# P5 copied by ScalarE and P3's bank opened with P1+P6+P5 by VectorE, in the seven-product sets of a fused attention and MLP kernel

## The chip, the cores and the metric

The kernel runs on one core of one Trainium2 chip. The metric is the device time of one execution in microseconds (us), the median of several runs. Its engines are named as in the profile: PE is TensorE (matmul), PEld its weight load, DVE is VectorE, ACT is ScalarE, POOL is GpSimd, SP is SyncE.

## The reference

Linear attention with a decay per head, in blocks along the sequence, and then a two-layer MLP on its output:

```python
# q, k, v: (4 batches, 8 heads, 768 positions, 64), lam: one decay per head
for b in range(nb):                                   # blocks along the sequence
    intra = einsum('bhic,bhjc->bhij', qb, kb) * Dmask
    intra = einsum('bhij,bhjd->bhid', intra, vb)
    inter = einsum('bhid,bhde->bhie', qb * lam_pow, kv_state)
    out[:, :, sl] = intra + inter
    kv_state = lam_block * kv_state + einsum('bhsd,bhse->bhde', kb * rev_pow, vb)
x = out.transpose(0, 2, 1, 3).reshape(3072, 512)
h = x @ w_in                                          # 512 -> 2048
g = h * tanh(softplus(h))                             # Mish
return g @ w_out                                      # 2048 -> 512
```

## The kernel before

The sequence is cut into six stages `n` = 0 to 5 of 128 positions by 4 batches, 512 tokens each. The instructions of each engine stand in the order in which the program writes them (a manual schedule), so an engine that waits holds back all that is queued behind it. A stage runs the first layer, then the second (`fast_unit`), and in between pieces of the attention of the stage after it (`pair_a`, `pair_s`, `pair_o`), placed by hand in the dictionary `visit`.

The hidden layer has 16 tiles of 128 features. In stages 2 to 5, tiles 0 to 7 are computed plainly by eight calls of `mm1_duo(n, g, ...)`: two tiles by 256 tokens, 8 products of 128x256, into a bank of the PSUM tag `ph` (two banks), read by one Mish on ACT into `hsg`. Below, "the plain unit (g, h)" is pair `g` of the tiles and half `h` of the tokens. Tiles 8 to 15 are computed by two "sets", `g` = 0 and 1 (`set_unit`), each a 2x2 blocked product done with seven block products instead of eight (Winograd's form). A block product is 4 products of 128x256. With sums of blocks of the input (`xsum`, four DVE additions) and of the weights (`isum`), a set computes

- P1 and P2; Mish(P1+P2) gives block (0,0),
- P5, kept in SBUF as `p5`,
- P6 on top of P1 in bank z: z = P1+P6,
- P7 on top: z = P1+P6+P7; Mish(z+P5) gives block (1,1) (the sum goes through the SBUF tile `hs`),
- P3 into bank y, which starts as a copy of P1+P6; Mish(P1+P6+P3+P5) gives block (0,1),
- P4 on top of z; Mish(z) gives block (1,0).

The banks of the two sets are given by `homes`: x, z, w, y of set 0 lie in tags pS, pS, po, pk, those of set 1 in pk, po, ph, ph. w holds P5. In the code x is `sx0`/`sx1` in the profile, z is `sz`, w is `sw`, y is `sy`, the copy of P1 is `u`, `p5` is `p`.

The stage's list `units` sets the order. Unit 4 is the plain unit (0,1), preceded by `pair_s` of the next stage, whose four mask products (DVE, L365, tile `sb`) read the banks that z and y take over; after unit 4 come the four `xsum`. Units 5 to 12 are the plain units (1,1) and (2,1) with the steps "hold" and "open" (ACT copies P1 back into bank z), P5 and P6 of set 0, P5 and P6 of set 1, the plain unit (3,1), P7, P3 and P4 of both sets, and last the step "late", the Mish of y. Unit 13 starts the second layer with its P1 (tile `x`, needs plain tiles only); P5 of the second layer (tile `w`, weights `gsum`) follows. `token_sum` (DVE, tile `gsum`, placed by `sums`) makes sums over blocks of `hsg`: `gsum0` in two parts from block (1,1) of the plain tiles and of block (1,0) of the sets, then `gsum1`, `gsum3` and `gsum2`.

Of the kernel before, what the change touches and what calls it, by code (L numbers as in the profile page):

```python
# [9 lines left out]
AF = mybir.ActivationFunctionType  # L10
# [10 lines left out]
def kernel(  # L21
# [10 lines left out]
    nc = tc.nc  # L32
    B, H, S, D = q.shape
    C = 128
    NG = S // C
# [41 lines left out]
    def load_v(i):  # L77
        nc.gpsimd.dma_start(out=vz[i % NVB][:, :, 0:D], in_=chunk_rows(v, i))  # L78
# [212 lines left out]
    def next_state(n, p):  # L291

        nc.vector.tensor_tensor(
            out=state[p][(n + 1) % 2], in0=raws[n, p],
            in1=lbc.unsqueeze(1).unsqueeze(3).broadcast_to([128, 2, JP, D]), op=ALU.mult)
# [112 lines left out]
    def pace():  # L408
        nc.gpsimd.tensor_copy(paced, mark[-1])  # L409
# [75 lines left out]
    def i_quarter(g, r, c):  # L485

        t = win[g - 2]
        return t[:, r * KH : (r + 1) * KH, c * 256 : (c + 1) * 256]
# [27 lines left out]
    first = {}  # L516
# [3 lines left out]
    def set_unit(n, g, step):  # L520

        def place(key):
            if (n, g, key) not in first:
                tag, bufs = homes[g][key]
                first[n, g, key] = ps.tile([128, 2, 2 * C], F32, name=f"s{key}{g}", tag=tag, bufs=bufs)
            return first[n, g, key]

        def kept(key):
            first[n, g, key] = work.tile([128, 2, 2 * C], F32, name=key, tag=key, bufs=2)
            return first[n, g, key]  # L530

        def mish(r, c, src):
            ni = NKI // 2 + 4 * g + 2 * c
            dst = hsg[n][:, ni : ni + 2, r * 2 * C : (r + 1) * 2 * C]
            nc.scalar.activation(dst, src, AF.Mish)
            mark.append(dst[0:1, 0, 0:1])

        def plus_p5(key, out):
            nc.vector.tensor_tensor(out=out, in0=first[n, g, key], in1=first[n, g, "p5"], op=ALU.add)

        def x_quarter(r, c):
            return lambda kk: xt[n][:, c * KH + kk, r * 2 * C : (r + 1) * 2 * C]

        def x_part(i):
            return lambda kk: xsum[n, i][:, kk, :]

        def w_quarter_(r, c):
            return lambda kk, m: i_quarter(g, r, c)[:, kk, m * 128 : (m + 1) * 128]

        def w_part_(i):  # L550
            return lambda kk, m: isum[g][i][:, kk, m * 128 : (m + 1) * 128]

        if step == "hold":
            place("w")
            return
        if step == "open":
            nc.scalar.activation(place("z"), first[n, g, "u1"], AF.Copy)
            return
        if step == "late":
            mish(0, 1, first[n, g, "y"])  # L560
            return
        key, lhs, rhs = {
            "P1": lambda: ("x", w_quarter_(0, 0), x_quarter(0, 0)),
            "P2": lambda: ("x", w_quarter_(1, 0), x_quarter(0, 1)),
            "P6": lambda: ("z", w_part_(1), x_part(1)),
            "P5": lambda: ("w", w_part_(0), x_part(0)),
            "P7": lambda: ("z", w_part_(2), x_part(2)),
            "P3": lambda: ("y", w_quarter_(1, 1), x_part(3)),
            "P4": lambda: ("z", w_part_(3), x_quarter(1, 1)),
        }[step]()  # L570
        t = place(key)
        for m in range(2):
            for kk in range(KH):
                nc.tensor.matmul(  # L574
                    t[:, m, :], lhs(kk, m), rhs(kk),
                    start=(step in ("P1", "P5") and m == 0 and kk == 0), stop=(kk == KH - 1),
                    skip_group_check=True)
        if step == "P1":
            nc.scalar.activation(kept("u1"), t, AF.Copy)
        elif step == "P2":  # L580
            mish(0, 0, t)
        elif step == "P5":
            nc.vector.tensor_copy(kept("p5"), t)  # L583
        elif step == "P6":
            nc.scalar.activation(place("y"), t, AF.Copy)
        elif step == "P7":
            o = work.tile([128, 2, 2 * C], F32, name="hs", tag="hs", bufs=2)
            plus_p5("z", o)
            mish(1, 1, o)
        elif step == "P3":  # L590
            plus_p5("y", t)
        elif step == "P4":
            mish(1, 0, t)

# [61 lines left out]
    p5 = {}  # L656
# [102 lines left out]
    units = [(mm1_unit, (0, ni)) for ni in range(NKI)]  # L759
# [3 lines left out]
    sums = {3: ((2, 0),), 7: ((2, 1),), 11: ((0, 0), (1, 0), (3, 0)), 15: ((0, 1), (1, 1)), 16: ((3, 1),)}  # L763
# [35 lines left out]
    for n in range(1, NG):  # L799
        r, s, t = Pair(), Pair(), Pair()  # L800
        r.n, r.bs, s.n, s.bs, t.n, t.bs = n, (2, 3), n + 1, (0, 1), n + 1, (2, 3)
        def duo(g, half):
            return mm1_duo, (n, g, half * (GT // 2), (half + 1) * (GT // 2))

        def part(g, *steps):
            return [(set_unit, (n, g, step)) for step in steps]

        later = []
        if 1 < n < NG - 1:
            later += [lambda i=(n + 1) * B + b: load_v(i) for b in range(B)]  # L810
        if n < NG - 2:
            later += [lambda f=f, i=(n + 2) * B + b: f(i) for b in range(B) for f in (load_k, load_q)]
        if n == 1:
            units = [[duo(g, half)] for half in range(2) for g in range(NKI // 2)]
            visit = {11: (pair_s, s), 16: (pair_o, s), 21: (pair_a, s), 26: (pair_s, t), 29: (pair_o, t)}
            turns = {1: 9, 4: 10, 7: 11, 23: 12, 25: 13}
            slots = range(8, 16)
            sums = {9: ((2, 0),), 11: ((2, 1),), 13: ((0, 0), (1, 0)), 15: ((0, 1), (1, 1)), 20: ((3, 0),), 21: ((3, 1),)}
        else:
            units = [part(0, "P1") + part(1, "P1") + [duo(0, 0)], part(0, "P2") + part(1, "P2") + [duo(1, 0)],  # L820
                     [duo(2, 0)], [duo(3, 0)],
                     [duo(0, 1)], part(0, "hold") + part(1, "open") + [duo(1, 1)], part(0, "open") + [duo(2, 1)],
                     part(0, "P5", "P6"), part(1, "P5") + [(duo_bank, (n, 3, 1))] + part(1, "P6"), [duo(3, 1)],
                     part(0, "P7") + part(1, "P7"), part(0, "P3") + part(1, "P3"),
                     part(0, "P4") + part(1, "P4") + part(0, "late") + part(1, "late")]
            visit = {}
            if n < NG - 1:
                visit = {0: (pair_a, r), 3: (pair_s, s), 13: (pair_o, s), 22: (pair_s, t), 25: (pair_o, t)}
            if n < NG - 2:
                visit[17] = pair_a, s  # L830
            turns = {1: (n + 1) * B + 2, 2: (n + 1) * B + 3, 20: (n + 2) * B, 23: (n + 2) * B + 1}
            slots = range(4, 16)
            sums = {8: ((2, 0),), 12: ((0, 0), (0, 1), (1, 0), (1, 1)), 14: ((2, 1),), 18: ((3, 0),), 19: ((3, 1),)}
        steps = ("P1", "P5", "P6", "P2", "P7", "P3", "P4")
        units += [[(fast_unit, (n, step, blk))] for step in steps for blk in range(2)]
        scales = []
        for u, calls in enumerate(units):
            for fn, args in calls:
                fn(*args)
            if n == 1 and u == 0:  # L840
                turn(8)
                look_s(7)
            if n == 1 and u == 2:
                f = look_kv(7)
                look_o(7)
                f()
                next_state(1, 1)
            for _ in range({0: 1, 1: 1, 2: 2, 3: 1, 4: 1}.get(u, 0) if n == 1 else 0):
                pace()
                ahead.pop(0)()  # L850
            if later and u in slots:
                pace()
                later.pop(0)()
            for i, part in sums.get(u, ()):
                token_sum(n, i, part)
            if turns.get(u, NG * B) < NG * B:
                turn(turns[u])
            if u in visit:
                f, s_ = visit[u]
                s_.spare = ("po", "po") if u < 13 else ("pS", "pk") if f is pair_a else ("ph", "po")  # L860
                if f is pair_o and s_ is s and n > 1:
                    f(s_, scales)
                else:
                    f(s_)
            if n > 1 and scales and u in (15, 16, 17, 19):
                scales.pop(0)()
            if n > 1 and u == 4:
                for i in range(4):
                    x_sum(n, i)
# [30 lines left out]
```

## Time and profile before

| | |
|---|---|
| median of 3 runs | 200.87 us (200.67 to 201.45) |
| the profiled execution | 202.27 us, of which the profile's span is 200.5 us |
| granted TensorE clock | 1.00 |
| busy in the span | PE 190.2 us (95%), PEld 157.4, DVE 149.6 (75%), ACT 111.3 (55%), POOL 78.8 |

A row of the timeline gives the start and the length in us, the engine, the line, the operation with what it writes and reads, how many instructions of the kind stand in a row, and in brackets the idle time before them with what ended it. The end of a matmul is modelled, so for PE the starts are read: rows of 8 products of 128x256 start 0.87 us apart when nothing holds them. Instructions of one group on ACT or DVE overlap their neighbours, since the next one starts before the one in front has written its last result.

### The profile page before, as it was taken

Reading aid. Unit: us, or ns where it says so; the run is one execution under the profiler, and the core shown is the slowest. Engines: PE = TensorE matmul, PEld = TensorE weight load, DVE = VectorE, ACT = ScalarE, POOL = GpSimd, SP = SyncE. Lnnn points to the kernel's source line nnn. Section 1 sums busy time; section 2 is a strip of 40 time slices with the busy share of each in tenths; the row PEclk is TensorE's granted clock in tenths of the full one; section 3 lists DMA queues with packets and bytes.
Section 4 is the critical chain, followed back from the end, with each engine's and each line's share of the span. In section 5 each row is a group of like instructions: output and inputs, shape, how many; then the busy total and the mean of one; then the engine's idle time right before and its main releaser. Section 6 shows DMA issues by size and latency. Waiting matters only on the chain.

```text
span 200.5 us, 5119 instructions
## 1 busy us (share of the span) xinstructions
PE 190.2 (95%) x2049; PEld 157.4 (79%) x2049; DVE 149.6 (75%) x287; ACT 111.3 (55%) x230; POOL 78.8 (39%) x129
## 2 busy tenths in 40 slices
PE   7976999999999999999999999999999999999993
PEld 3643446878898998987998987998987988888882
DVE  7887679899944978888969787969787928237813
ACT  5693575242665431467791557780666880786530
POOL 7996333679396810008870008870008000000000
PEclk9999999999999999999999999999999999999999
DMA  8999999999999998659999869999759714500014
GB/s 129 144 146 185 207 206 200 157 168 170 205 119 172 168 134 181 173 94 92 128 112 195 167 142 99 134 122 182 224 99 115 47 26 134 157 3 2 0 56 157
DMA packets 112458, 26.82 MB, mean 134 GB/s; under 512 B 101554, under 2 KB 112434, under 8 KB 112434
## 3 DMA queue, kind: packets, MB, share of 16 engines
q0 software_dynamic: 77552, 13.37, 94.0%
q1 hardware_dynamic: 30848, 9.97, 26.6%
q10 hardware_dynamic: 4034, 3.15, 5.3%
q8 instruction: 16, 0.26, 0.6%
q14 instruction: 8, 0.07, 0.1%
HBM read 27.26 MB, written 6.29 MB: 167 GB/s over the span
## 4 chain that ended last, share of the span: by engine, by line
PE 80%; DVE 8%; DMA 5%; POOL 4%; issue 1%; ACT 0%; DVEq 0%; POOLq 0%
PE ph L453 17%; PE z L626 14%; PE x L626 10%; PE ph L418 7%; PE y L626 5%; PE w L626 5%; PE sz L574 4%; DMA vz<-in_v_dram 4%; PE sx L574 3%; PE pS L349 2%; DVE sb L365 2%; DVE p L583 2%; PE pO L376 2%; PE sy L574 2%; DVE xsum L514 1%; POOL kn L67 1%
## 5 line engine op out<-in xcount | busy, mean ns | idle before, releaser
L453 PE MATMUL ph<-xt,win 128*128 128x256 f16 x384 | 45.0, 273 | 1.6 <-DVE p L583 1.4
L453 PEld LDWEIGHTS <-win 128*128 128x128 f16 x384 | 37.1, 98 | 6.8 <-issue 2.4
L626 PEld LDWEIGHTS <-gsum 128*128 128x128 f16 x384 | 36.9, 98 | 4.8 <-DVE tsum L480 0.3
L460 ACT ACTIVATE hsg<-ph 128x512 f16<-128x512 f32 x48 | 28.7, 597 | 15.6 <-PE ph L453 15.3
L409 POOL COPY paced<-hsg 1x1 f16<-1x1 f16 x42 | 9.8, 233 | 56.4 <-ACT hsg L460 55.9
L626 PEld LDWEIGHTS <-hsg 128*128 128x128 f16 x272 | 26.0, 98 | 3.2
L626 PE MATMUL x<-wout,hsg 128*128 128x256 f16 x192 | 23.7, 273 | 0.0
L626 PE MATMUL z<-tsum,gsum 128*128 128x256 f16 x192 | 23.6, 273 | 0.0
L67 POOL DMA_DIRECT2D kn<-in_k_dram x23 | 20.6, 894 | 6.3 <-DMA win<-in_moe_w_in_dram 2.1
L78 POOL DMA_DIRECT2D vz<-in_v_dram x24 | 21.2, 887 | 4.4 <-DMA wout<-in_moe_w_out_dram 1.7
L75 POOL DMA_DIRECT2D qn<-in_q_dram x23 | 20.4, 887 | 6.0 <-DMA wout<-in_moe_w_out_dram 3.6
L365 DVE TENSOR_TENSOR sb<-pS,maskT 128x512 f16<-128x512 f32 x32 | 19.8, 682 | 1.9 <-PE pS L349 1.8
L612 DVE TENSOR_TENSOR gsum<-hsg 128x1024 f16<-128x1024 f16 x24 | 16.2, 687 | 4.8 <-ACT hsg L460 2.8
L683 ACT ACTIVATE osum<-z 128x512 f32<-128x512 f32 x5 | 3.0, 597 | 25.1 <-PE z L626 25.1
L265 DVE TENSOR_TENSOR ktil<-kn,lk 128x512 f16<-128x512 f16 (+1 forms) x22 | 14.6, 683 | 2.5 <-DMA kn<-in_k_dram 2.5
L288 DVE TENSOR_TENSOR raw<-pv,state 64x256 f32<-64x256 f32 x24 | 10.1, 422 | 8.0 <-PE pv L328 7.6
L418 PE MATMUL ph<-xt,win 128*128 128x512 f16 x64 | 14.5, 379 | 0.3 <-ACT xt L257 0.3
L574 PEld LDWEIGHTS <-isum 128*128 128x128 f16 x128 | 12.4, 97 | 2.3 <-issue 0.3
L430 ACT ACTIVATE hsg<-ph 128x512 f16<-128x512 f32 x16 | 9.6, 597 | 5.8 <-PE ph L418 5.8
L653 DVE TENSOR_TENSOR osum<-z,p 128x512 f32<-128x512 f32 x6 | 4.1, 689 | 10.8 <-issue 6.0
L626 PE MATMUL y<-wout,gsum 128*128 128x256 f16 x96 | 11.8, 273 | 0.0
L418 PEld LDWEIGHTS <-win 128*128 128x128 f16 x64 | 6.1, 97 | 7.3 <-issue 0.5
(114 smaller groups left out, 320.2 us busy)
## 6 DMA issues: line engine op xcount, KB each, us to landing
vz<-in_v_dram POOLq DMA_DIRECT2D x24, 128.0 KB, 4.6
out_dram<-osum SPq DMA_DIRECT2D x12, 256.0 KB, 2.9
kn<-in_k_dram POOLq DMA_DIRECT2D x23, 128.0 KB, 5.5
qn<-in_q_dram POOLq DMA_DIRECT2D x23, 128.0 KB, 6.0
out_dram<-osum ACTq DMA_DIRECT2D x11, 256.0 KB, 3.1
wout<-in_moe_w_out_dram POOLq DMA_DIRECT2D x4, 512.0 KB, 16.8
win<-in_moe_w_in_dram POOLq DMA_DIRECT2D x3, 512.0 KB, 11.2
win<-in_moe_w_in_dram POOLq DMA_DIRECT2D x2, 256.0 KB, 7.3
```

What stands on the lines that cost most here:

```text
L67: nc.gpsimd.dma_start(out=kn[i], in_=chunk_rows(k, i))
L75: nc.gpsimd.dma_start(out=qn[i], in_=chunk_rows(q, i))
L78: nc.gpsimd.dma_start(out=vz[i % NVB][:, :, 0:D], in_=chunk_rows(v, i))
L265: (nc.gpsimd if B + 1 < i < 2 * B else nc.vector).tensor_tensor(out=t, in0=kn[i], in1=bc(lk, 2, D), op=ALU.mult)
L288: nc.vector.tensor_tensor(out=raw[rs, b % 2, j0 : j0 + nj, :], in0=pv[rs, :, rs], in1=olds(rs), op=ALU.add)
L365: nc.vector.tensor_tensor(out=s.sb[m][t], in0=sc[m][t], in1=bc(maskT, 1, JP), op=ALU.mult)
L418: nc.tensor.matmul(ph_t[ni][:, lo:hi], w_in(ni, kc), xt[n][:, kc, lo:hi], start=(kc == 0), stop=(kc == NKC - 1),)
L453: nc.tensor.matmul(t[:, m, lo - half * h : hi - half * h], w_in(ni, kc), xt[n][:, kc, lo:hi], start=(m == 0 and kc == 0), stop=(kc == NKC ...
L460: nc.scalar.activation(hsg[n][:, 2 * g : 2 * g + 2, half * h : half * h + h], t, AF.Mish)
L574: nc.tensor.matmul(t[:, m, :], lhs(kk, m), rhs(kk), start=(step in ("P1", "P5") and m == 0 and kk == 0), stop=(kk == KH - 1), skip_group_c ...
L612: nc.vector.tensor_tensor(out=gsum[n, i][:, ks, :], in0=a, in1=b, op=op)
L626: nc.tensor.matmul(places(n, key)[:, blk, lo:hi], lhs(kk, blk), rhs(kk, lo, hi), start=(fresh and kk == 0 and blk == 0), stop=(kk == HK - ...
```

## The change

In stages 2 to 5:

- P5 is copied out of bank w by ACT instead of DVE.
- Bank y is no longer a copy of P1+P6 made by ACT. A new step "mid", on DVE, writes P1+P6+P5 into it (`plus_p5("z", place("y"))`). P3 is then added by PE, and Mish reads the bank directly; the in-place addition of P5 on DVE after P3, and the step "late", go.
- The order: "open" of set 0 comes before "open" of set 1, "hold" goes; then P5 of both sets, P6 of set 0, "mid" of set 0, P6 of set 1, the plain unit (3,1), "mid" of set 1, and P7, P3, P4. The bank of the plain unit (3,1) is now the one left by the plain unit (2,1), not the one that held P5 of set 1.
- The Mish operations on ACT are in the order hs, hs, sy, sy, sz, sz; before it was hs, hs, sz, sz, sy, sy.
- The first part of `gsum2` moves from unit 8 to unit 9, where DVE does it between "mid" of set 1 and the first `hs`.
- In stage 5 the plain unit (1,0) comes before P2 of the two sets instead of after.

```diff
-        if step == "hold":
-            place("w")
-            return
         if step == "open":
             nc.scalar.activation(place("z"), first[n, g, "u1"], AF.Copy)
             return
-        if step == "late":
-            mish(0, 1, first[n, g, "y"])
+        if step == "mid":
+            plus_p5("z", place("y"))
             return
...
         elif step == "P5":
-            nc.vector.tensor_copy(kept("p5"), t)
-        elif step == "P6":
-            nc.scalar.activation(place("y"), t, AF.Copy)
+            nc.scalar.activation(kept("p5"), t, AF.Copy)
...
         elif step == "P3":
-            plus_p5("y", t)
+            mish(0, 1, t)
...
-                     [duo(0, 1)], part(0, "hold") + part(1, "open") + [duo(1, 1)], part(0, "open") + [duo(2, 1)],
-                     part(0, "P5", "P6"), part(1, "P5") + [(duo_bank, (n, 3, 1))] + part(1, "P6"), [duo(3, 1)],
+                     [duo(0, 1)], part(0, "open") + [duo(1, 1)], part(1, "open") + [duo(2, 1)],
+                     part(0, "P5") + part(1, "P5"), part(0, "P6", "mid") + part(1, "P6"), [duo(3, 1)] + part(1, "mid"),
                      part(0, "P7") + part(1, "P7"), part(0, "P3") + part(1, "P3"),
-                     part(0, "P4") + part(1, "P4") + part(0, "late") + part(1, "late")]
+                     part(0, "P4") + part(1, "P4")]
+            if n == NG - 1:
+                units[0] += units[1].pop(),
...
-            sums = {8: ((2, 0),), 12: ...
+            sums = {9: ((2, 0),), 12: ...
```

More of the change, by code (lines that the diff above doesn't have):

```diff
@@ L832 @@
             slots = range(4, 16)
-            sums = {8: ((2, 0),), 12: ((0, 0), (0, 1), (1, 0), (1, 1)), 14: ((2, 1),), 18: ((3, 0),), 19: ((3, 1),)}
+            sums = {9: ((2, 0),), 12: ((0, 0), (0, 1), (1, 0), (1, 1)), 14: ((2, 1),), 18: ((3, 0),), 19: ((3, 1),)}
         steps = ("P1", "P5", "P6", "P2", "P7", "P3", "P4")
```

## The prediction

> **What bounds the kernel now.** I read the page first, then the waits, then the timeline of the part of a stage that the change touches.
>
> ```profile
> span 200.5 us, 5119 instructions
> ...
> PE 190.2 (95%) x2049; PEld 157.4 (79%) x2049; DVE 149.6 (75%) x287; ACT 111.3 (55%) x230; POOL 78.8 (39%) x129
> ```
>
> ```profile
> PE ph L453 <- DVE p L583: 1.4, 4, 0.4
> ```
>
> PE is busy 95% of the span, so only what makes PE wait, or lets it start sooner, moves the end. The last row (us in total, times, longest) is such a wait: the plain unit (3,1) waits in each of the four stages for DVE's copy of P5 of set 1, whose bank it takes. The timeline shows its whole price. This is stage 4:
>
> ```profile
> 148.05 2.48 DVE L365 TENSOR_TENSOR sb<-pS,maskT 128x512 f16<-128x512 f32 x4 [0.59 <-PE pS L349]
> ...
> 149.26 0.60 ACT L460 ACTIVATE hsg<-ph 128x512 f16<-128x512 f32 x1 [1.17 <-PE ph L453]
> 149.76 0.60 ACT L557 ACTIVATE sz<-u 128x512 f32<-128x512 f32 x1
> ...
> 150.91 0.60 PE L574 MATMUL sw<-xsum,isum 128*128 128x256 f16 x4
> ...
> 151.28 0.60 ACT L460 ACTIVATE hsg<-ph 128x512 f16<-128x512 f32 x1
> ...
> 151.41 0.60 PE L574 MATMUL sz<-xsum,isum 128*128 128x256 f16 x4
> ...
> 151.91 1.28 DVE L583 COPY p<-sw 128x512 f32<-128x512 f32 x2
> 152.09 0.58 ACT L585 ACTIVATE sy<-sz 128x512 f32<-128x512 f32 x1 [0.22 <-ACT hsg L460]
> 152.28 0.60 PE L574 MATMUL sz<-xsum,isum 128*128 128x256 f16 x4
> ...
> 153.11 0.68 DVE L612 TENSOR_TENSOR gsum<-hsg 128x1024 f16<-128x1024 f16 x1
> 153.24 1.03 PE L453 MATMUL ph<-xt,win 128*128 128x256 f16 x8 [0.36 <-DVE p L583]
> ...
> 154.11 1.04 PE L574 MATMUL sz<-xsum,isum 128*128 128x256 f16 x8
> ...
> 154.81 1.29 DVE L539 TENSOR_TENSOR hs<-sz,p 128x512 f32<-128x512 f32 x2 [1.02 <-issue]
> ...
> 155.53 1.23 ACT L535 ACTIVATE hsg<-hs 128x512 f16<-128x512 f32 x2 [0.62 <-DVE hs L539]
> ...
> 155.86 1.04 PE L574 MATMUL sz<-xt,isum 128*128 128x256 f16 x8
> ...
> 156.67 1.07 ACT L535 ACTIVATE hsg<-sz 128x512 f16<-128x512 f32 x2
> ...
> 157.28 1.29 DVE L612 TENSOR_TENSOR gsum<-hsg 128x1024 f16<-128x1024 f16 x2
> ...
> 157.62 1.09 ACT L535 ACTIVATE hsg<-sy 128x512 f16<-128x512 f32 x2
> ...
> 158.84 3.48 PEld L626 LDWEIGHTS <-gsum 128*128 128x128 f16 x32
> ...
> 158.95 1.91 PE L626 MATMUL w<-tsum,gsum 128*128 128x256 f16 x16
> ```
>
> The 8 products at 153.24 take until 154.11: 0.87 us, so 4 take 0.44. The last 4 before them start at 152.28 and should be followed at 152.72; the plain unit starts at 153.24, 0.52 late. A further 0.06 lies at 150.91 to 151.41. From 153.24 PE runs on without a gap to `w`, the second layer's P5, 5.71 us later. It can do so because the first `gsum`, which `w` needs, starts at 157.28 and is written by 157.97, 0.87 before its weight load at 158.84. That slack decides what the change is worth.
>
> **The steps measured here**, all for tiles of 128x512. From the start of 4 products to the DVE operation that reads them 0.70 (154.11 to 154.81), to an ACT one 0.68 (151.41 to 152.09). DVE: start to start 0.60 (two copies from 151.91, the next at 153.11), 0.69 each by the rows below. ACT: start to start 0.505 in the first chain (149.26 to 151.28, four steps). From the start of `hs` on DVE to its Mish 0.72 (154.81 to 155.53), of which 0.03 is beyond its length. The second Mish follows the second `hs`, 0.60 later (156.13); the next comes 0.54 after (156.67), then 0.475 each (156.67 to 157.62, two). From the start of the first `sz` Mish to the first `gsum` 0.61 (156.67 to 157.28). From the start of a `gsum` to the `w` product that waits for it I take 0.84: 0.69 for itself, 0.04 to reach PE (the second copy starts at 152.51, ends at 153.20, PE goes at 153.24), 0.11 from weight load to product (158.84 to 158.95).
>
> ```profile
> L583 DVE COPY p<-sw 128x512 f32<-128x512 f32 x8 | 5.3, 685 | 3.5 <-PE sw L574 3.4
> L539 DVE TENSOR_TENSOR sy<-sy,p 128x512 f32<-128x512 f32 x8 | 5.2, 690 | 0.0
> L585 ACT ACTIVATE sy<-sz 128x512 f32<-128x512 f32 x8 | 4.7, 582 | 2.1 <-PE sz L574 1.2 <-ACT hsg L460 0.9
> L672 ACT ACTIVATE p<-w 128x512 f32<-128x512 f32 x6 | 3.6, 598 | 4.2 <-PE w L626 4.2
> ```
>
> **What each edit costs by itself.** DVE loses eight copies of 685 ns (5.3 us in all); the eight "mid" additions replace the eight in-place additions at the same price: 685 to 690 ns bounds an addition from one bank into another from both sides. ACT swaps eight copies of 582 ns (bank to bank) for eight of 598 ns (bank to SBUF, the row of the second layer's `p`). PE does the same products. Neither engine's total bounds the time, so the worth lies in the order. The Trainium skill, ScalarE: Activation LUTs, Step-by-step: what each stage is for, says that a ScalarE write to PSUM is faster than one to SBUF, which speaks against moving ACT's copy there. By the rows that is 16 ns a copy, two copies a stage, 0.13 us over the kernel if all of it showed; the sum below takes 0.60 for the copy.
>
> **Stage 4, step by step.** The third mask product (DVE, L365) starts at 148.05 + 2 x 0.60 = 149.25 and ends at 149.94. Bank z of set 0 is the one it reads, so "open" of set 0, now first behind the Mish of 149.26, waits for it: 149.97, against 149.76 for the "open" that stood there. Behind it on ACT are queued two Mish operations, the other "open" and then P5's copy, four steps of 0.505: the copy starts at 151.99 and ends at 152.59. PE: P5 of both sets from 150.91, P6 of set 0 at 151.78 (8 products later), P6 of set 1 at 152.22, the plain unit (3,1) at 152.66. Its bank is that of the plain unit (2,1), whose Mish, one step ahead of P5's copy, ends at about 152.1: no wait. So the plain unit starts 0.58 sooner (153.24 to 152.66); the DVE copy that it waited for is gone.
>
> What is late next: "mid" of set 0 needs P5's copy (152.59 + 0.03 = 152.62) and P6 (151.78 + 0.70 = 152.48): it starts at 152.62 and ends at 153.31; "mid" of set 1 starts at 153.22 and ends at 153.91. P7 of set 0 comes at 153.53, of set 1 at 153.97: both find their banks read, the second by a hair. `gsum2` goes third on DVE, 153.82, and the first `hs` fourth, 154.42 (P7 alone would allow 153.53 + 0.70 = 154.23). P4 of set 1 at 155.71 meets the second `hs` ending at 155.71: 0.04 at most.
>
> On ACT follow the Mish of hs at 154.42 + 0.72 = 155.14, hs 155.74, sy 156.28, sy 156.76, sz 157.23, sz 157.71. The two sy now stand ahead of the sz for which the first `gsum` waits. It starts at 157.23 + 0.61 = 157.84, later by 0.56 than before, although PE is 0.58 ahead. `w` would be due at 152.66 + 5.71 = 158.37; it starts at 157.84 + 0.84 = 158.68. After 4 products (0.44) it needs the second half of `gsum0`, 0.61 behind the first (DVE's x2 row at 157.28 with 0.68 each): another 0.17. So `w` counts as started at 158.85, against 158.95: **the stage gains 0.10 of the 0.58**. Put shortly, `w` starts 4.43 after the first `hs`. Behind `w` nothing moves: P6 of the second layer, 1.75 later, finds `gsum1` written.
>
> ```profile
> 88.60 2.48 DVE L365 TENSOR_TENSOR sb<-pS,maskT 128x512 f16<-128x512 f32 x4 [0.59 <-PE pS L349]
> 93.80 1.03 PE L453 MATMUL ph<-xt,win 128*128 128x256 f16 x8 [0.37 <-DVE p L583]
> 99.50 1.69 PE L626 MATMUL w<-tsum,gsum 128*128 128x256 f16 x14
> ...
> 118.22 2.49 DVE L365 TENSOR_TENSOR sb<-pS,maskT 128x512 f16<-128x512 f32 x4 [0.59 <-PE pS L349]
> 121.21 0.60 PE L574 MATMUL sw<-xsum,isum 128*128 128x256 f16 x4
> 123.62 1.03 PE L453 MATMUL ph<-xt,win 128*128 128x256 f16 x8 [0.34 <-DVE p L583]
> 129.33 1.91 PE L626 MATMUL w<-tsum,gsum 128*128 128x256 f16 x16
> ...
> 177.30 0.60 ACT L460 ACTIVATE hsg<-ph 128x512 f16<-128x512 f32 x1 [0.28 <-PE ph L453]
> ...
> 178.85 0.60 PE L574 MATMUL sw<-xsum,isum 128*128 128x256 f16 x4
> 181.26 1.03 PE L453 MATMUL ph<-xt,win 128*128 128x256 f16 x8 [0.34 <-DVE p L583]
> ...
> 186.50 1.69 PE L626 MATMUL w<-tsum,gsum 128*128 128x256 f16 x14
> ```
>
> One more row for the other stages is from the chain of waits that ended last, in stage 5 (start, length):
>
> ```profile
> 172.70 1.07 PE sx L574 x8
> ```
>
> **The other stages.** Stage 2 has stage 4's distances (88.60, 93.80, 99.50 are each 59.45 before): 0.10. In stage 3 the mask products lie earlier against PE: "open" at 118.22 + 1.20 + 0.69 + 0.03 = 120.14, P5's copy 122.16 to 122.76, "mid" 122.79, `hs` 1.80 later 124.59, `w` 129.02 against 129.33: 0.31 of the 0.66 that PE gains before the plain unit (123.62 to 121.21 + 1.75 = 122.96). Stage 5 has no mask products. There P2's 8 products take 1.07 instead of 0.87, waiting for ACT's copy of P1; the plain unit (1,0) now covers that, and all behind moves up by 0.20 or 0.21: P5 at 178.64, the plain unit at 180.39, 0.87 sooner. ACT: Mish at 177.09, "open" 177.60, Mish 178.11, "open" 178.61, Mish 179.12, P5's copy 179.62, "mid" 180.25, `hs` 182.05, `w` 186.48 against 186.50: 0.02. Only the second layer's P1 lies before `w` there, so the wait is longest.
>
> Sum: 0.10 + 0.31 + 0.10 + 0.02 = 0.53 us. The profiled execution (202.27, span 200.5) would become 201.74; the median of the runs, 200.87, which is 1.40 below that execution, becomes **200.3**. Six chained distances of about 0.02 each in four stages make it 200.3 within 0.5.
>
> **The rivals.** *The wait does not come back*: the same gap stands four times on PE, a bank frees it, and the sums arrive in time. Then 0.58 + 0.66 + 0.58 + 0.87 = 2.69 are gained, 198.2 us; the bound of 0.5% (below) is passed if `w` waits 0.12 a stage less than worked out. The Trainium skill, Perfetto Trace Analysis, Optimization Strategy, says that the same bubble repeating on the engine that should be saturated can mean too few buffers, by which freeing the bank would recover it whole. The 0.5 us gap in all four stages fits that. Against it: ACT cannot begin the first of six Mish operations before `hs`, and `hs` cannot start before P7 + 0.70, so with everything ahead of it free the chain shortens by only 0.19 in stages 2 and 4 (154.42 to 154.23), 0.06 in stage 3 (124.59 to 122.96 + 0.87 + 0.70) and 0.09 in stage 5 (182.05 to 180.39 + 0.87 + 0.70): 1.06 in all with the 0.53. 0.20, since each measured distance may be off.
>
> *ACT's queue costs more than the bank gives*: "open" of set 0 stands first and waits for the third mask product, with two Mish operations and P5's copy behind it, and the two sy stand ahead of the sz. If ACT's start-to-start were its 0.60 length in both chains, that adds 4 x 0.095 + 0.06 + 2 x 0.125 = 0.69 to the way to the first `gsum`, 2.8 in four stages, and 0.53 less makes 203.1 us. It turns slower than before from 0.13 a stage, and passes the bound of 0.5% from 0.38. For it: a first copy into a bank behind a wait isn't in these rows in this order. Against it: both cadences are measured on the same shapes. 0.12.
>
> *The plain unit still waits*, for the Mish of the unit (2,1) instead of a copy: by the sum that ends at 152.1, 0.5 before it is wanted. That would leave about 200.9, inside the forecast's case.
>
> **How the numbers follow.** A difference of 0.5% (1.0 us) is about what a measurement of this kernel can tell from no change. The forecast, 0.53 faster within 0.5, lies inside it: same 0.68. Faster by more 0.20, slower by more 0.12. The range 199.2 to 201.4 leaves out the far part of the faster case (0.08) and the slower case beyond 201.4 (0.12). The forecast's own range is 199.8 to 200.8.
>
> **What would show it.** Right: no wait of PE on P5's copy at L453, the plain unit (3,1) directly behind P6; a new idle of PEld before `w`, ended by DVE's `gsum`, of 0.3 to 0.7 a stage; sz Mish as the last of six, and `gsum` directly behind it. Wrong: `w` following the second layer's P1 without a gap (first rival), or PE idle before P7 with DVE's "mid" as its releaser (second).

## The result and the profile after

The changed kernel takes 200.61 us (median, 200.0 to 201.23), the kernel before 201.24 in the same comparison: a ratio of 0.9966 with a 95% interval of 0.9952 to 0.9981, that is 0.7 us faster (0.4 to 1.0). The forecast was 0.53 us faster, and 200.3 us within 0.5. A second comparison, e8 below, gave 0.9976 (0.9954 to 0.9998).

The page and the waits (us in total, times, longest) of the changed kernel:

```profile
span 199.1 us, 5098 instructions
...
PE 191.6 (96%) x2049; PEld 157.5 (79%) x2049; DVE 144.8 (73%) x279; ACT 110.8 (56%) x230; POOL 80.8 (41%) x129
```

```profile
PEld L621 <- DVE gsum L607: 2.7, 8, 0.7
...
PE w L621 <- DVE gsum L607: 0.4, 1, 0.4
```

The wait of PE on P5's copy is gone from the list. In its place stands the wait of the weight load on `gsum`, twice in each of the four stages: the second layer's P5 is now held. The timeline of stage 4, the rows that answer to those of before:

```profile
146.93 2.49 DVE L365 TENSOR_TENSOR sb<-pS,maskT 128x512 f16<-128x512 f32 x4 [0.59 <-PE pS L349]
...
148.14 0.60 ACT L460 ACTIVATE hsg<-ph 128x512 f16<-128x512 f32 x1 [1.17 <-PE ph L453]
...
148.91 0.60 ACT L554 ACTIVATE sz<-u 128x512 f32<-128x512 f32 x1 [0.17 <-DVE sb L365]
...
149.80 1.03 PE L571 MATMUL sw<-xsum,isum 128*128 128x256 f16 x8
...
150.67 1.04 PE L571 MATMUL sz<-xsum,isum 128*128 128x256 f16 x8
150.92 1.08 ACT L580 ACTIVATE p<-sw 128x512 f32<-128x512 f32 x2
...
151.54 1.04 PE L453 MATMUL ph<-xt,win 128*128 128x256 f16 x8
151.55 1.30 DVE L539 TENSOR_TENSOR sy<-sz,p 128x512 f32<-128x512 f32 x2 [0.67 <-ACT p L580]
...
152.41 1.08 PE L571 MATMUL sz<-xsum,isum 128*128 128x256 f16 x8
...
152.75 0.68 DVE L607 TENSOR_TENSOR gsum<-hsg 128x1024 f16<-128x1024 f16 x1
...
153.33 1.04 PE L571 MATMUL sy<-xsum,win 128*128 128x256 f16 x8
153.35 1.28 DVE L539 TENSOR_TENSOR hs<-sz,p 128x512 f32<-128x512 f32 x2
...
154.07 1.23 ACT L535 ACTIVATE hsg<-hs 128x512 f16<-128x512 f32 x2 [0.86 <-DVE hs L539]
...
155.21 1.07 ACT L535 ACTIVATE hsg<-sy 128x512 f16<-128x512 f32 x2
...
156.16 1.09 ACT L535 ACTIVATE hsg<-sz 128x512 f16<-128x512 f32 x2
...
156.79 1.29 DVE L607 TENSOR_TENSOR gsum<-hsg 128x1024 f16<-128x1024 f16 x2 [2.16 <-ACT hsg L535]
157.54 0.33 PEld L621 LDWEIGHTS <-gsum 128*128 128x128 f16 x4 [0.32 <-DVE gsum L607]
157.54 2.08 PE L621 MATMUL w<-tsum,gsum 128*128 128x256 f16 x16
...
158.14 2.95 PEld L621 LDWEIGHTS <-gsum 128*128 128x128 f16 x28 [0.27 <-DVE gsum L607]
...
159.47 1.91 PE L621 MATMUL z<-tsum,gsum 128*128 128x256 f16 x16
```

The plain unit (3,1) at 151.54 follows P6 (150.67) after 8 products' 0.87 us: no gap. DVE stands idle for 2.16 us before `gsum`, since ACT does the two sy (155.21) ahead of the sz (156.16) that `gsum` reads; with the sz first (e1 below) it is 1.18. PE's weight load waits twice.

**Measured by stage.** What stands ahead of the first set differs between profiles by more than the change moves: P1 of stage 2 starts at 82.16 before, 81.46 after, and between 80.83 and 83.22 in the experiments, although no edit touches what lies ahead of it. So the kernels are compared by the distances between the starts of P1 (`sx`) of stages 2 to 5, and in stage 5 from P1 to the second layer's P6. These are the rows of the changed kernel:

```profile
81.46 1.04 PE L571 MATMUL sx<-xt,win 128*128 128x256 f16 x8
...
110.97 1.04 PE L571 MATMUL sx<-xt,win 128*128 128x256 f16 x8
...
140.49 1.04 PE L571 MATMUL sx<-xt,win 128*128 128x256 f16 x8
...
169.56 1.04 PE L571 MATMUL sx<-xt,win 128*128 128x256 f16 x8
...
186.91 0.82 PE L621 MATMUL z<-tsum,gsum 128*128 128x256 f16 x6
```

All kernels, in us, with the timed ratio beside them (its 95% interval in brackets):

| kernel | stage 2 | 3 | 4 | 5 | sum against before | timed ratio |
|---|---|---|---|---|---|---|
| before | 29.62 | 29.83 | 29.18 | 17.46 | | |
| changed | 29.51 | 29.52 | 29.07 | 17.35 | -0.64 | 0.9966 (0.9952, 0.9981) |
| e8: changed, again | 29.51 | 29.51 | 29.06 | 17.35 | -0.66 | 0.9976 (0.9954, 0.9998) |
| e1: Mish of sz first | 29.13 | 29.14 | 28.68 | 16.59 | -2.55 | 0.9888 (0.985, 0.9927) |
| e2: gsum2 behind hs | 29.22 | 29.21 | 29.35 | 17.23 | -1.08 | 0.9932 (0.9896, 0.9968) |
| e3: stage 5 in the old order | 29.51 | 29.51 | 29.07 | 17.55 | -0.45 | 0.9983 (0.9965, 1.0001) |
| e4: P5 copied by DVE | 29.95 | 29.94 | 29.50 | 17.60 | +0.90 | 1.0051 (1.0025, 1.0078) |
| e5: before, other bank only | 29.10 | 29.10 | 28.65 | 16.95 | -2.29 | 0.9898 (0.9861, 0.9936) |
| e6: e1 and e2 | 29.09 | 29.09 | 28.63 | 16.60 | -2.68 | 0.9868 (0.9842, 0.9894) |
| e7: e5 and stage 5's order | 29.10 | 29.10 | 28.68 | 16.75 | -2.46 | 0.9878 (0.9842, 0.9913) |
| e9: open in the old order | 29.35 | 29.33 | 28.90 | 17.35 | -1.16 | 0.9967 (0.9948, 0.9985) |

The sums of the stages and the ratios (1% is 2.0 us) agree within the intervals, save for e9, which falls just outside. There is one profile for each kernel (two for the changed one, which agree within 0.01 a stage), and two waits for the DMA of `xt` are in the table that no edit touches. One, of 0.17 us, stands in stage 3 of the kernel before, which is 0.21 longer than its stage 2; in every other kernel stages 2 and 3 agree within 0.02. All sums count these 0.21. Without them the change gains 0.43 and e9 0.95, which lies within its interval (0.3 to 1.05). The other, of 0.63 us, stands in stage 4 of e2.

### The profile page after: what moved, and what is told of

The parts are those of the page before. It is cut to its first block, busy times and chain, and to the rows that moved or that the text cites. A ratio compares the mean times of both kernels' runs of the same rounds, so it can differ in the third digit from the quotient of the medians.

```text
span 199.1 us, 5098 instructions
## 1 busy us (share of the span) xinstructions
PE 191.6 (96%) x2049; PEld 157.5 (79%) x2049; DVE 144.8 (73%) x279; ACT 110.8 (56%) x230; POOL 80.8 (41%) x129
## 4 chain that ended last, share of the span: by engine, by line
PE 88%; ACT 5%; DVE 4%; issue 1%; ACTq 0%
PE ph L453 20%; PE z L621 14%; PE x L621 10%; PE ph L418 7%; PE w L621 6%; PE y L621 6%; PE sz L571 4%; PE sx L571 4%; PE pS L349 2%; PE pO L376 2%; PE pO L255 2%; PE sw L571 1%; ACT hsg L535 1%; PE pv L328 1%; PE sy L571 1%; PE busy L157 1%
## 5 line engine op out<-in xcount | busy, mean ns | idle before, releaser
L621 PEld LDWEIGHTS <-gsum 128*128 128x128 f16 x384 | 36.2, 98 | 7.3 <-DVE gsum L607 2.7
L409 POOL COPY paced<-hsg 1x1 f16<-1x1 f16 x42 | 11.9, 284 | 54.8 <-ACT hsg L460 54.5
L621 PE MATMUL w<-tsum,gsum 128*128 128x256 f16 x96 | 12.2, 273 | 0.6 <-DVE gsum L607 0.4
```

Source lines behind the costliest of these rows:

```text
L621: nc.tensor.matmul(places(n, key)[:, blk, lo:hi], lhs(kk, blk), rhs(kk, lo, hi), start=(fresh and kk == 0 and blk == 0), stop=(kk == HK - ...
```

## The experiments

**e1: where the gain went.** The changed kernel with the Mish of y behind P4 again:

```diff
+        if step == "late":
+            mish(0, 1, first[n, g, "y"])
+            return
...
         elif step == "P3":
-            mish(0, 1, t)
...
-                     part(0, "P4") + part(1, "P4")]
+                     part(0, "P4") + part(1, "P4") + part(0, "late") + part(1, "late")]
```

> The changed kernel, with the Mish of y put back behind P4 (step late), so that ACT does hs, hs, sz, sz, sy, sy. Theory A (the bank's gain is taken back because two sy Mish stand on ACT ahead of the two sz for which the first gsum, and with it the second layer's P5, waits): the chain from the first hs to P5 of the second layer is 0.95 us shorter a stage, P5 is no longer held, and 2.6 us against before are gained (stage gains 0.58, 0.66, 0.58, 0.87 less 0.04 each in two of them), about 2.0 more than the change. Theory B (the chain is bound by where hs starts, through the P5 copy and gsum2 on DVE, and ACT's order is only a part): P5 still held, at most 0.2 a stage more than the change, 1.2 to 1.4 us against before.

Measured: ratio 0.9888, 2.3 us; the stages show 2.55. Stage 4 of e1, by the timeline:

```profile
151.96 1.28 DVE L539 TENSOR_TENSOR hs<-sz,p 128x512 f32<-128x512 f32 x2
...
153.81 1.06 ACT L535 ACTIVATE hsg<-sz 128x512 f16<-128x512 f32 x2
154.42 1.29 DVE L608 TENSOR_TENSOR gsum<-hsg 128x1024 f16<-128x1024 f16 x2 [1.18 <-ACT hsg L535]
154.76 1.08 ACT L535 ACTIVATE hsg<-sy 128x512 f16<-128x512 f32 x2
...
155.83 2.72 PEld L622 LDWEIGHTS <-gsum 128*128 128x128 f16 x25
155.94 1.91 PE L622 MATMUL w<-tsum,gsum 128*128 128x256 f16 x16
```

`gsum` starts 2.46 after `hs` (3.44 in the changed kernel) and is written 0.72 before its weight load at 155.83, which no longer waits. Theory A holds, B falls: ACT's order alone held back 1.9 of the 2.55 us. The timed ratios say the same, as the intervals of e1 and of the changed kernel lie apart.

**e5: the bank alone.** The kernel before, with the banks of two tiles exchanged: the plain unit (3,1) and bank y of set 1. P6 of set 1 leaves its copy into y out (a step "copy" behind the unit makes it), and the unit's Mish is held back so that ACT keeps its order:

```diff
-    def mm1_duo(n, g, lo, hi):
+    def mm1_duo(n, g, lo, hi, later_mish=None):
...
+        if step == "copy":
+            nc.scalar.activation(place("y"), first[n, g, "z"], AF.Copy)
+            return
...
-                     part(0, "P5", "P6"), part(1, "P5") + [(duo_bank, (n, 3, 1))] + part(1, "P6"), [duo(3, 1)],
+                     part(0, "P5", "P6"), part(1, "P5", "P6"),
+                     [(mm1_duo, (n, 3, GT // 2, GT, held))] + part(1, "copy") + [(lambda held=held: held.pop()(), ())],
```

> The kernel before, with one thing changed: the plain unit (3,1) takes the bank left by the plain unit (2,1), and bank y of set 1 the one left by P5 of set 1 (the copy of z into y is written behind the unit's products and ahead of its Mish). All operations and ACT's order as before. Theory A: the unit follows P6 without a gap, the 0.50 to 0.52 us of each stage are gained, and the second layer's P5 is not held, since sz stands ahead of sy on ACT: 2.0 us faster than before, three times what the whole change gives. Theory B (what follows is bound by hs anyway): PE is held at P5 of the second layer instead, 0.5 us or less.

Measured: ratio 0.9898, 2.1 us; by the stages 0.52, 0.73, 0.53 and 0.51. Stage 4:

```profile
150.22 0.60 PE L582 MATMUL sz<-xsum,isum 128*128 128x256 f16 x4
150.66 1.04 PE L453 MATMUL ph<-xt,win 128*128 128x256 f16 x8
...
154.09 1.06 ACT L540 ACTIVATE hsg<-sz 128x512 f16<-128x512 f32 x2
...
154.70 1.29 DVE L621 TENSOR_TENSOR gsum<-hsg 128x1024 f16<-128x1024 f16 x2
...
156.26 0.75 PEld L635 LDWEIGHTS <-gsum 128*128 128x128 f16 x7
```

The unit comes 0.44 behind the last four products, and `gsum` (written by 155.39) lies 0.87 ahead of its load. Two exchanged banks, with one copy written later and no operation added, removed or given to another engine, give three times what the whole change gives. The old wait was worth its full 0.5 us a stage, as long as the order of the Mish operations stayed. Stage 3's 0.73 holds the 0.21 of the DMA's wait: 0.12 lies ahead of P5, the rest between P5 and P6.

**e4: who copies P5.** The changed kernel with `nc.vector.tensor_copy(kept("p5"), t)`.

> The changed kernel, with P5 copied by DVE again (all else as changed). Theory A: two copies of 0.60 stand on DVE ahead of mid, gsum2 and hs, so hs starts 0.45 us later in stages 2 to 4 and 0.26 in stage 5, P7 waits 0.3 for mid, and all of it reaches the end: 1.6 us slower than the change, 1.0 slower than before. Rival (which engine copies P5 is immaterial, the bank and the order do it all): as the change, 0.6 faster than before.

Measured: ratio 1.0051, 1.0 us slower than before. By the stages 0.44, 0.42, 0.43 and 0.25 more than the change, where 0.45 and 0.26 were expected. Stage 4:

```profile
152.47 1.04 PE L571 MATMUL sw<-xsum,isum 128*128 128x256 f16 x8
...
153.41 1.28 DVE L580 COPY p<-sw 128x512 f32<-128x512 f32 x2
...
154.61 1.29 DVE L539 TENSOR_TENSOR sy<-sz,p 128x512 f32<-128x512 f32 x2
...
156.40 1.29 DVE L539 TENSOR_TENSOR hs<-sz,p 128x512 f32<-128x512 f32 x2
```

`hs` starts 3.93 after P5 (153.35 - 149.80 = 3.55 in the changed kernel), 0.38 later; the other 0.05 of this stage lies ahead of P5 (152.47 is 9.36 behind P1, against 9.31). In stages 2, 3 and 5 `hs` is 0.43, 0.43 and 0.24 later. In the new order the copy's place on ACT is needed: what `hs` is late by is paid in full, since the second layer's P5 is what waits for it.

**e2: the sum that moved with it.** The changed kernel with `sums = {10: ((2, 0),), ...}`: `gsum2` behind both hs.

> The changed kernel, with the first part of gsum2 moved from unit 9 to unit 10, behind both hs. Theory A: hs starts when P7 allows, 0.19, 0.06, 0.19 and 0.09 us sooner in stages 2 to 5, and all of it reaches the second layer's P5, which is what is waited for: 0.5 us more than the change, 1.1 to 1.2 against before. Rival (ACT's six Mish are bound by ACT or by P3 and P4, not by the first hs): no more than the change, 0.6 against before.

Measured: ratio 0.9932, 1.4 us. Stages 2, 3 and 5 are 0.29, 0.31 and 0.12 shorter than the change; stage 4 shows a wait of 0.63 us for the DMA of `xt` that the change's profile doesn't have, and can't be compared:

```profile
147.19 2.78 PE L453 MATMUL ph<-xt,win 128*128 128x256 f16 x24 [0.63 <-DMA xt<-xtok]
```

Theory A holds in kind, and was low. In stage 2 of e2 `hs` starts 0.64 after P7, not the 0.70 worked out; in the changed kernel it starts 0.94 after P7 (94.32 and 93.38), not 0.89. So it is 0.30 sooner, where 0.19 was expected, and the stage is 0.29 shorter:

```profile
93.41 1.08 PE L571 MATMUL sz<-xsum,isum 128*128 128x256 f16 x8
...
94.05 1.29 DVE L539 TENSOR_TENSOR hs<-sz,p 128x512 f32<-128x512 f32 x2 [0.21 <-PE sz L571]
```

In stage 3 0.06 was expected, as the mask products were taken to lie earlier there than in stage 2; without the DMA's wait of before they don't, and stage 3 gains what stage 2 gains. The timed intervals of e2 and of the changed kernel overlap, so this rests on the stages.

**e3: stage 5's order.** The changed kernel without `units[0] += units[1].pop(),`.

> The changed kernel, with the plain unit (1,0) of stage 5 put back behind P2 of the sets. Theory A: P2 waits 0.2 us for ACT's copies of P1 again, all that follows in stage 5 starts from there, so 0.2 slower than the change and 0.4 to 0.5 faster than before; stages 2 to 4 keep their lengths of 29.5, 29.5 and 29.1 us between their P1. Rival (the second layer's P5 is held in stage 5 anyway, so the 0.2 is hidden): as the change.

Measured: ratio 0.9983, against 0.9976 for the changed kernel beside it (201.04 and 201.03 us), which can't tell 0.2 us. The traces can: stage 5 is 17.55 us, 0.20 longer, and the others as in the change. P2's 8 products start at 171.28, 1.03 after the plain unit, and the next starts 0.92 later:

```profile
170.25 1.04 PE L453 MATMUL ph<-xt,win 128*128 128x256 f16 x8
171.28 1.09 PE L571 MATMUL sx<-xt,win 128*128 128x256 f16 x8
172.20 5.40 PE L453 MATMUL ph<-xt,win 128*128 128x256 f16 x48
```

**e6 and e7: the best of both.** e6 is e1 with e2's place of `gsum2`; e7 is e5 with stage 5's order of the change.

> The kernel of e1 (Mish of y behind P4) with the first part of gsum2 in unit 10, behind both hs. Theory A: the second layer's P5 isn't held any more in e1, so the earlier hs only takes away what P4 waits for hs in stages 2 to 4 (its 8 products 0.92 instead of 0.87 us): 0.1 us or nothing on top of e1's 2.3 to 2.5 against before. Rival (the two are independent and add up): 0.5 more than e1.

> The kernel of e5 (before, the plain unit (3,1) on the bank left by (2,1)) with stage 5's plain unit (1,0) ahead of P2, as in the change. Theory A: the 0.2 us of P2's wait in stage 5 come on top: 2.2 to 2.3 us faster than before.

Measured: 0.9868 (198.99 us) and 0.9878 (198.8 us), 2.7 and 2.5 us faster than before, which the timing doesn't tell apart. By the stages e6 is 0.13 shorter than e1, not 0.5: with the second layer's P5 no longer held, an earlier `hs` is worth only what P4 waited for the second `hs` (in stage 4 P4's 8 products take 0.87, 153.46 to 154.33, against 0.92 in e1, 152.81 to 153.73). P7 takes 0.92 in both. e7 is 0.17 shorter than e5, all of it in stage 5 (16.95 to 16.75, with 0.03 lost in stage 4).

**e8: the changed kernel again.**

> The changed kernel as it is, beside the others on the same chip: 0.6 us faster than before by its trace (stages of 29.5, 29.5, 29.1 us between their P1, against 29.6, 29.8, 29.2, and 0.1 in stage 5).

Measured: ratio 0.9976, 0.5 us; by the stages 0.66, each within 0.01 of the first profile.

**e9: open behind the third mask product.** The changed kernel with `part(1, "open") + [duo(1, 1)], part(0, "open") + [duo(2, 1)]`.

> The changed kernel, with the two steps open in the old order (set 1 first), so that ACT doesn't stand behind the third mask product at the head of its queue. Theory A: in stages 2 to 4 P5's copies leave ACT 0.28 us sooner, mid is then bound by P6 and starts 0.18 sooner, and hs and the second layer's P5 with it: 0.5 us faster than the change, 1.1 faster than before; stage 5, without mask products, keeps its length. Rival (ACT catches up behind open, the place of open is immaterial): as the change, 0.6 faster than before.

Measured: the stages are 0.16, 0.19, 0.17 and 0.00 shorter than the change, as expected; the timed ratio is 0.9967, 0.7 us, which neither shows the 0.5 nor excludes it. Stage 4:

```profile
148.78 0.60 ACT L554 ACTIVATE sz<-u 128x512 f32<-128x512 f32 x1
...
149.94 1.03 PE L571 MATMUL sw<-xsum,isum 128*128 128x256 f16 x8
...
150.77 1.09 ACT L580 ACTIVATE p<-sw 128x512 f32<-128x512 f32 x2
...
151.52 1.30 DVE L539 TENSOR_TENSOR sy<-sz,p 128x512 f32<-128x512 f32 x2 [0.50 <-PE sz L571]
```

P5's copy starts 0.83 after P5 (1.12 in the changed kernel), and "mid", now released by P6, 1.58 after it (1.75). The mechanism is in the trace; that it moves the time by 0.5 us isn't shown.

## Why the prediction was right, step by step

- **The wait and its end.** The plain unit (3,1) follows P6 at once in all four stages. e5 shows that the gap was worth what the timeline said, about 0.5 (0.52, 0.53 and 0.51 in stages 2, 4 and 5).
- **What is late next.** The chain named, P5's copy on ACT, "mid", `gsum2`, `hs`, six Mish, `gsum`, is the one in the trace. From P5 to `hs` 3.51 was worked out for stage 4, 3.55 measured; from `hs` to the first product of `w` 4.26 and 4.19 (153.35 to 157.54); the second wait 0.17 and 0.18 (159.47 - 157.54 - 1.75). Stage 4 gained 0.11 against 0.10, stage 2 the same. That it is so close is in part luck, as two small errors cancel. The first "open" was put 0.03 behind the end of the third mask product and comes about 0.09 behind it (148.91, against 146.93 + 1.20 + 0.69 = 148.82). And from the start of `gsum` to `w` 0.84 was taken, 0.11 of it from weight load to product; where the load itself waits, load and product start together (157.54), and it is 0.75 (156.79 to 157.54).
- **Stage 5** gained 0.11, not 0.02. The terms are the same surplus between `hs` and `w`, here 0.08, and 0.02 ahead of `hs`; there is no mask product here to cancel them:

```profile
177.42 1.04 PE L571 MATMUL sw<-xsum,isum 128*128 128x256 f16 x8
...
180.81 1.28 DVE L539 TENSOR_TENSOR hs<-sz,p 128x512 f32<-128x512 f32 x2
...
184.99 2.09 PE L621 MATMUL w<-tsum,gsum 128*128 128x256 f16 x16 [0.42 <-DVE gsum L607]
```

  `hs` is 3.39 after P5 (3.41 worked out), `w` 4.18 after `hs` (4.26).
- **Stage 3** came out at the forecast's 0.31, but about 0.2 of it lies in the kernel before and not in the change. From P5 (`sw`) to the second layer's P6 the gain is 0.20 (121.21 to 131.08 before, the 129.33 of `w` and 1.75; 120.28 to 129.95 after). The other 0.12 lies ahead of P5 (9.43 and 9.31 from P1): before, PE waited there for the DMA of `xt`, after it didn't. The forecast took the mask products' lead over P5 in stage 3 (121.21 - 118.22 = 2.99) as fixed; it held that wait, and is 2.87 after (120.28 - 117.41). The row of before (stage 3's plain unit (0,1), with the idle time in brackets):

```profile
118.59 2.78 PE L453 MATMUL ph<-xt,win 128*128 128x256 f16 x24 [0.17 <-DMA xt<-xtok]
```

  From P5 on the sum is 0.11 + 0.20 + 0.11 + 0.11 = 0.53. That this is the forecast's figure is luck: stage 5 gave 0.09 more and stage 3 0.11 less. Had the kernel before not waited for the DMA, stage 3 would by its stage 2 have gained 0.10, and the whole 0.43 (an estimate: 29.62 in place of 29.83). One profile of before can't say how often it waits there.
- **The small waits.** P4 was to wait at most 0.04 for the second `hs`; P7, whose wait was put at nothing ("by a hair"), and P4 take 0.92 and 0.91 in place of 0.87 in stages 2 to 4 (152.41 to 153.33, 154.21 to 155.12). They cost nothing there, since the second layer's P5 is held behind them; e6 against e1 shows P4's as 0.13 us in all.
- **ACT's copy.** The groups of the changed kernel have it at 604 ns, 22 more than the copy into PSUM (582) that it replaces:

```profile
L580 ACT ACTIVATE p<-sw 128x512 f32<-128x512 f32 x8 | 4.3, 604 | 0.0
```

  The rule of the Trainium skill that writing to PSUM is faster for ScalarE (ScalarE: Activation LUTs, Step-by-step: what each stage is for) agrees in sign. e4 shows that it doesn't decide who should copy: the copy on VectorE, whose queue is on the chain, costs 1.5 us more by the stages.
- **The rivals.** The first (the wait doesn't come back) didn't occur in the change, but is what e1 shows once ACT's order is put back: 2.55 us by the stages where 2.69 was worked out. The rule of the Trainium skill weighed with it, that a repeated bubble can mean too few buffers (Perfetto Trace Analysis, Optimization Strategy), points at the right place: e5 gains the whole gap with the banks alone. But e5 adds no buffer, two tiles only exchange theirs, so too few buffers isn't what the gap showed. The change gained about a quarter of e5's, as the new ACT order let PE wait at another place. The second rival (ACT slower than its cadence) is excluded by the cadences: open to P5's copy 4 steps in 2.01 us (148.91 to 150.92), sy to sz two steps in 0.95 (155.21 to 156.16). The third (the plain unit still waits) didn't occur either.

## What to carry to other kernels

When a wait of the bound engine is removed, look for the slack of the next thing that it needs, here 0.87 us at `gsum`, and ask whether the same edit makes that later: an order on a second engine that is busy only 56% of the span took back three quarters of the gain. Among operations that become ready together on such an engine, do those first that somebody waits for soonest, even if that keeps a bank longer. And try the smallest part of a change alone: here the exchange of two banks, in e5, was worth more than the whole.

## What the runs showed that was not expected

Whether PE waits for the DMA of `xt` differs between profiles: 0.17 us in stage 3 before, none in the changed kernel, 0.63 in stage 4 of e2. The part ahead of the sets, which no edit touches, ends between 80.83 and 83.22 us. Both make a single profile's span a poor measure of a change below 1 us: e9's span equals the changed kernel's 199.1, while its stages are 0.5 shorter. The distances between recurring instructions are steadier, but a single wait for a DMA can move them too, as in stage 3 of the kernel before. What sets the time of that first part, and when PE waits for the DMA, wasn't studied.
